# Retention followed by channel mix on one core: k transposed by head pairs, mu loaded as rows, block 0 split into parts, the last output tile by columns

## The chip, the cores and the metric

The kernel runs on one core of a Trainium2 chip. The core has a matrix engine (PE, with PEld for its weight loads), a vector engine (DVE), an activation engine (ACT), a general engine (POOL) and a queue engine (SP). Each engine takes its own instructions in program order and waits on semaphores for the others. Transfers between main memory and the on-chip memory are issued from SP, ACT or POOL; POOL's transfers here also convert float32 to float16. PE writes to PSUM, eight banks of 128 partitions by 2 KB, and DVE and ACT read them.

The metric is device time in microseconds (us) of one execution, as the median of several runs.

## What is computed

Two stages. The first is a retention recurrence over batch 4, 8 heads, 768 tokens, head size 64; the second is a channel mix with a shifted input, a squared relu and a sigmoid gate. The output is float32.

```python
# q, k, v: (4, 8, 768, 64)
gamma = 1.0 - 2.0 ** (-5.0 - np.arange(H))
for t in range(S):
    state = gamma[None, :, None, None] * state + np.einsum('bhd,bhe->bhde', k[:, :, t], v[:, :, t])
    y[:, :, t] = scale * np.einsum('bhd,bhde->bhe', q[:, :, t], state)
# x = y as (4, 768, 512); w_k: (512, 1024), w_v: (1024, 512), w_r: (512, 512)
x_prev = np.concatenate([np.zeros((B, 1, D)), x[:, :-1, :]], axis=1)
xk = mu_k * x + (1.0 - mu_k) * x_prev
xr = mu_r * x + (1.0 - mu_r) * x_prev
k = np.maximum(xk @ w_k, 0.0)
v = k * k @ w_v
r = 1.0 / (1.0 + np.exp(-(xr @ w_r)))
return r * v
```

## The kernel before

The 3072 tokens are cut into 12 blocks of 256 (three to a batch). Each block is two chunks u = 0, 1 of 128 tokens. A chunk's tokens lie two to a partition (index i), so that 64 partitions hold one chunk and 128 the block. The recurrence is done by chunks: inside a chunk by masked scores, between chunks by a decayed state.

Every step is a short function, called by a code in one long hand-over table, the string `ORDER` (lines 16 to 63). A word such as `X.0.0.1.2` is a code and its arguments; the digits behind `@` are the PSUM banks that the step uses. The table sets the order on every engine; what waits for what is put in as semaphores from the data. The first argument is the block n in all of them:

- `lk`, `lq`, `lv` (lines 169 to 179) load k, q and v. Loads of q and v go out on POOL, those of k on SP or, with a 2 behind the block, on POOL. `wk`, `wr`, `wv` load the weights on POOL, in halves for wk and wv; `mu` (393) loads the two mixing vectors on ACT, one value to a partition and column.
- `gy` (404) builds a decay table on DVE by a copy and seven doublings. `ks` (181) scales k into float16 by 128x1024 elements, on DVE (0) or POOL (1).
- `T` (195) transposes on PE by 64x64 pieces, 32 for q (0) and 32 for k (1), into two shared banks; `E` (207) copies the result out on ACT.
- `S` (222) makes the scores for i = 0, 1; `M` (234) masks them on DVE, 128x1024 each. `C` (244) makes each chunk's state product, `U` (262) adds it to the state on DVE, `G` (272) decays it on POOL. `I` (278) applies the state to q, `Y` (290) adds the masked scores times v, `D` (310) scales the result into xT on DVE.
- `dx` (318) takes the difference to the token before, on DVE or POOL. `X.n.w.j0.j1` (325) forms xk (w = 0) and xr (w = 1) on DVE, one 128x256 instruction for each j of 4.
- `K` (334) multiplies xk with w_k: four groups g of two, 8 matmuls of 256 columns each. `Q` (344) takes relu and square on ACT. `R` (351) makes the gate product by 128 tokens, 4 matmuls of 512; `s` (358) its sigmoid on ACT. `V` (363) multiplies with w_v by halves, 4 matmuls of 512 columns. `O` (370) joins gate and value on DVE, 128x512, and `st` (376) stores 256 KB from SP.
- `z` (397) are matmuls of zeros, whose results nothing reads.

Products of the same block are accumulated in PSUM, and rings of 2 to 6 buffers hold the tiles between the steps. All steps of block n+1's retention stand among the channel mix of block n.

## Time and profile before

| | us |
|---|---|
| median of 3 runs | 170.39 |
| lowest and highest of them | 169.95, 171.98 |
| profiled execution | 169.35 |
| its span, first to last instruction | 167.3 |

The profile shows one execution. A line of its timeline has the start and length in us, the engine, the source line, the operation with what it writes and reads, and in brackets how long the engine had stood idle and what ended that. Instructions of one kind that follow each other are merged, with their count; the length then runs from the first start to the last end. Ends of matmuls are modelled, so the distance between two starts tells more than a length. The chain of waits is followed back from the last instruction; "issue" in it is time in which an engine waited for nothing that the profile shows. In a table of windows, an engine's entry is its busy time in that stretch, with the number of instructions behind it, and PEclk is the granted share of PE's clock.

### The profile page before, as it was taken

What the parts mean: (1) busy time and instruction counts of PE and PEld (TensorE: products, weight loads), DVE (VectorE), ACT (ScalarE), POOL (GpSimd) and SP (SyncE); (2) the same over time, 40 slices, a digit from 0 to 9 for tenths busy, and PEclk for the clock granted to TensorE, in tenths of its full rate; (3) what the DMA queues carried; (4) which work ended last, traced back from release to release, by engine and by line L of the source; (5) the groups of instructions that cost most, each with busy time, mean ns of one, the idle gap of its engine ahead of it and who ended that gap; (6) DMA issues with size and microseconds to landing.
All of it is one profiled execution on the core that took longest, in us unless ns stands there. A gap on an engine that the chain in (4) does not pass through costs nothing.

```text
span 167.3 us, 6065 instructions
## 1 busy us (share of the span) xinstructions
PE 152.2 (91%) x2717; PEld 96.2 (57%) x2717; DVE 120.3 (72%) x194; ACT 93.5 (56%) x146; POOL 78.2 (47%) x75
## 2 busy tenths in 40 slices
PE   7884799989498969999999999999999999999990
PEld 2344446647365826756747756676566767566640
DVE  2676999696586999877877967977678699670311
ACT  3133009918145826776658738937657649286660
POOL 7984369395956952926809609114024140400000
PEclk9999579999789999999999999999999999999999
DMA  4999999999999991796569271630030030101303
GB/s 129 244 198 195 255 195 215 244 235 277 239 211 237 291 212 45 222 113 149 59 63 175 28 117 67 67 125 4 0 127 8 4 129 0 58 24 48 125 0 125
DMA packets 39529, 22.01 MB, mean 132 GB/s; under 512 B 26832, under 2 KB 35664, under 8 KB 39504
## 3 DMA queue, kind: packets, MB, share of 16 engines
q0 software_dynamic: 28464, 12.06, 53.2%
q1 hardware_dynamic: 9696, 9.44, 18.0%
q10 hardware_dynamic: 1344, 0.13, 1.2%
q8 instruction: 21, 0.34, 0.9%
q14 instruction: 4, 0.03, 0.0%
HBM read 24.25 MB, written 6.29 MB: 182 GB/s over the span
## 4 chain that ended last, share of the span: by engine, by line
PE 75%; DVE 9%; issue 5%; DMA 4%; ACT 2%; POOL 2%; DVEq 0%; POOLq 0%
PE ps L339 23%; PE ps L365 20%; PE ps L353 13%; DVE xr L329 5%; PE ps L228 4%; DMA k<-in_k_dram 4%; PE ps L298 4%; PE ps L202 4%; DVE a L236 3%; PE ps L399 2%; PE ps L255 2%; PE ps L285 2%; ACT k L349 1%; ACT kr L346 1%; DVE os L371 1%
## 5 line engine op out<-in xcount | busy, mean ns | idle before, releaser
L339 PE MATMUL ps<-xk,wk 128*128 128x256 f16 x384 | 47.8, 276 | 0.0
L365 PE MATMUL ps<-wv,k 128*128 128x512 f16 x192 | 44.6, 382 | 0.2 <-ACT k L349 0.2
L346 ACT ACTIVATE kr<-ps 128x512 f32<-128x512 f32 x48 | 28.4, 592 | 28.9 <-PE ps L339 28.9
L339 PEld LDWEIGHTS <-wk 128*128 128x128 f16 x384 | 37.0, 99 | 9.4 <-issue 0.2
L236 DVE TENSOR_TENSOR a<-ps,c_sb 128x1024 f16<-128x1024 f32 x24 | 28.5, 1219 | 10.5 <-PE ps L228 9.8
L349 ACT ACTIVATE k<-kr 128x512 f16<-128x512 f32 x48 | 30.3, 631 | 1.5
L365 PEld LDWEIGHTS <-k 128*128 128x128 f16 x192 | 18.6, 99 | 20.7 <-ACT k L349 2.1
L371 DVE SCALAR_TENSOR_TENSOR os<-ps,rs 128x512 f32<-128x512 f32 x24 | 16.4, 688 | 19.1 <-PE ps L365 8.0
L273 POOL TENSOR_TENSOR tg<-t,csm_sb 128x256 f16<-128x256 f32 x16 | 10.1, 629 | 37.0 <-DVE t L270 31.7
L353 PE MATMUL ps<-wr,xr 128*128 128x512 f16 x96 | 24.6, 380 | 1.9 <-DVE xr L329 1.4
L329 DVE SCALAR_TENSOR_TENSOR xr<-dx,mur,xT 128x256 f16<-128x256 f32 x48 | 25.3, 584 | 0.0
L320 POOL TENSOR_TENSOR dx<-xT 128x1024 f32<-128x1024 f32 x10 | 18.9, 1891 | 10.1 <-DVE xT L312 10.1
L359 ACT ACTIVATE rs<-ps 128x512 f32<-128x512 f32 x24 | 14.2, 590 | 16.8 <-PE ps L353 16.8
L329 DVE SCALAR_TENSOR_TENSOR xk<-dx,muk,xT 128x256 f16<-128x256 f32 x48 | 22.7, 533 | 1.1 <-POOL dx L320 1.0
L211 ACT COPY qT<-ps 128x1024 f16<-128x1024 f16 x12 | 12.1, 1010 | 19.1 <-PE ps L202 19.0
L183 POOL TENSOR_TENSOR ks<-k,csm_sb 128x1024 f16<-128x1024 f32 x10 | 19.3, 1927 | 0.9 <-POOL tg L273 0.8
L312 DVE TENSOR_TENSOR xT<-ps,gy_sb 128x1024 f32<-128x1024 f32 x12 | 14.7, 1223 | 3.4 <-PE ps L298 2.5
L170 POOL DMA_DIRECT2D q<-in_q_dram x12 | 10.9, 912 | 11.9 <-PE ps L202 9.9
L353 PEld LDWEIGHTS <-xr 128*128 128x128 f16 x96 | 8.6, 97 | 9.7 <-DVE xr L329 1.9
L228 PE MATMUL ps<-qT,kT 64*64 64x128 f16 x384 | 11.7, 227 | 2.6 <-issue 2.4
L170 POOL DMA_DIRECT2D v<-in_v_dram x12 | 11.0, 917 | 3.9 <-DMA wr<-in_moe_w_r_dram 2.1
L228 PEld LDWEIGHTS <-kT 64*64 64x64 f16 x384 | 8.2, 108 | 7.7 <-issue 4.5
(32 smaller groups left out, 119.2 us busy)
## 6 DMA issues: line engine op xcount, KB each, us to landing
out_dram<-os SPq DMA_DIRECT2D x24, 256.0 KB, 3.1
k<-in_k_dram SPq DMA_DIRECT2D x6, 512.0 KB, 4.7
q<-in_q_dram POOLq DMA_DIRECT2D x12, 256.0 KB, 8.6
v<-in_v_dram POOLq DMA_DIRECT2D x12, 256.0 KB, 6.8
k<-in_k_dram POOLq DMA_DIRECT2D x6, 512.0 KB, 13.8
wk<-in_moe_w_k_dram POOLq DMA_DIRECT2D x2, 512.0 KB, 10.6
wv<-in_moe_w_v_dram POOLq DMA_DIRECT2D x2, 512.0 KB, 17.1
wr<-in_moe_w_r_dram POOLq DMA_DIRECT2D x1, 512.0 KB, 13.7
```

Source lines behind the costliest of these rows:

```text
L170: eng.dma_start(out=d(n)[:, 2 * j0 : 2 * j1], in_=rows(x, n)[:, 2 * j0 : 2 * j1])
L183: (nc.vector, nc.gpsimd)[e].tensor_tensor(out=KS(n)[:, h0:h1].rearrange("p h (i d) -> p (h i) d", i=2), in0=K32(n)[:, h0:h1].rearrange("p ...
L228: nc.tensor.matmul(pa[u * D : u * D + D, hp, j, :], lhsT=KT(n)[r, u, j, i, :], rhs=QT(n)[r, u, j, :], start=(j == 0), stop=(j == NJ - 1), ...
L236: nc.vector.tensor_tensor(out=t[:, i], in0=pairs(banks("S", n, i)), in1=causal[:, i, None, None, :].to_broadcast([P, 2, NJ, C]), op=ALU.mult,)
L320: (nc.vector, nc.gpsimd)[e].tensor_tensor(out=DX(n)[:, j0:j1], in0=x[:, j0:j1, c : c + TM], in1=x[:, j0:j1, c - 1 : c + TM - 1], op=ALU.su ...
L329: nc.vector.scalar_tensor_tensor(out=XM[w](n)[:, j], in0=DX(n)[:, j], scalar=mu[:, j : j + 1], in1=x[:, j, c - 1 : c + TM - 1], op0=ALU.mu ...
L339: nc.tensor.matmul(pz[:, i, :], lhsT=wk16[:, co, fo * P : fo * P + P], rhs=XM[0](n)[:, co, :], start=(i == 0 and co == 0), stop=(co == NCO ...
L346: nc.scalar.activation(out=kr, in_=banks("K", n, g).rearrange("p (i t) -> p i t", i=2), func=AF.Relu)
L349: nc.scalar.activation(out=K2(n)[:, 2 * g : 2 * g + 2], in_=kr, func=AF.Square)
L353: nc.tensor.matmul(banks("R", n, tb), lhsT=XM[1](n)[:, co, tb * P : tb * P + P], rhs=wr16[:, co, :], start=(co == 0), stop=(co == NCO - 1),)
L365: nc.tensor.matmul(banks("V", n, tb, 0), lhsT=K2(n)[:, fo, tb * P : tb * P + P], rhs=wv16[:, fo, :], start=(fo == 0), stop=(fo == NFO - 1),)
L371: nc.vector.scalar_tensor_tensor(out=OS(2 * n + tb), in0=banks("V", n, tb, 0), scalar=1.0 / (KSC * KSC), in1=RS(2 * n + tb), op0=ALU.mult, ...
```

## The change

Five things are changed, and the table `ORDER` is written anew for all twelve blocks (its first words are shown in the diff).

1. *k by head pairs.* The scaled k lies as (i, head, d) and not as (head, i, d). One transpose takes a pair of heads, 128 tokens' partitions by 128 columns, so that a block's k takes 8 transposes of 128x128 and not 32 of 64x64. It lands in a bank of its own and is copied by its own step. q is still transposed by 64x64 (`Tq`), into two banks.
2. *mu from rows.* The two vectors are loaded as 4 rows of 128 each, transposed on PE (`mt`) and copied by ACT (`me`). They go out on ACT ahead of the first copies.
3. *Block 0 up to the scores by halves of heads.* Its k is loaded, scaled, transposed, copied, scored and masked in two halves (`.0.2` and `.2.4`).
4. *Block 0 from y to the key products by chunks.* `Du`, `du`, `Xu`, `Ku` and `Qu` do a chunk of 128 tokens each. A `Ku` is 16 matmuls of 128 columns.
5. *The last tile by columns.* The values, the result and the store of the last 128 tokens go by two halves of 256 columns, the stores from SP and ACT.

All loads of k behind block 0's go out on POOL. wk's first half is issued right behind v of block 0, and wk, wr and wv stand ahead of block 2's loads. The scaling of block 2's k is moved from POOL to DVE. There are 38 matmuls of zeros and not 29.

```diff
-lk.0 lq.0 lv.0 gy lk.1.2 lq.1 lv.1 wk.0 ks.0.0 wk.1 z.13@0 T.0.0@01 wr T.0.1 lk.2.2 E.0.0 C.0@23
...
+lk.0.0.0.2 lk.0.0.2.4 lq.0 mu lv.0 gy wk.0 lk.1.2 ks.0.0.0.2 z.7@0 mt@0 lq.1 me ks.0.0.2.4
+T.0.1.0.2@1 lv.1 E.0.1.0.2 T.0.1.2.4@0 E.0.1.2.4 wk.1 z.2@2 Tq.0@23 wr E.0.0 wv.0 z.4@4
...
-    gk_np = gam[None, :, None] ** (C - 1 - tok[:, None, :])
+    gk_np = gam[None, None, :] ** (C - 1 - tok[:, :, None])
...
-    KS = ring("ks_", 3, [H, 2 * D], F16)
-    QT = ring("qT_", 3, [2, NJ, C], F16)
-    KT = ring("kT_", 3, [2, NJ, 2, D], F16)
+    KS = ring("ks_", 3, [2, H, D], F16)
+    QT = ring("qT_", 3, [NJ, 2, C], F16)
+    KT = ring("kT_", 3, [NJ, 2, C], F16)
...
-            out=KS(n)[:, h0:h1].rearrange("p h (i d) -> p (h i) d", i=2),
-            in0=K32(n)[:, h0:h1].rearrange("p h (i d) -> p (h i) d", i=2),
-            in1=gk[:, 2 * h0 : 2 * h1, None].to_broadcast([P, 2 * (h1 - h0), D]),
+            out=KS(n)[:, :, h0:h1],
+            in0=K32(n)[:, h0:h1].rearrange("p h (i d) -> p i h d", i=2),
+            in1=gks[:, :, h0:h1, None].to_broadcast([P, 2, h1 - h0, D]),
...
     def trans(n, a, j0=0, j1=NJ):
-        pt, src = turned(n), (Q16, KS)[a](n)
+        pt = turned(n, a, j0).rearrange("p (j i t) -> p j i t", j=NJ, i=2)
         for j in range(j0, j1):
+            for i in range(2):
+                if a:
+                    nc.tensor.transpose(
+                        pt[:, j, i], KS(n)[:, i, 2 * j : 2 * j + 2].rearrange("p h d -> p (h d)"),
+                        ident,
+                    )
...
-    def scores(n, i):
-        pa = pairs(banks("S", n, i))
-        for j in range(NJ):
+    def scores(n, i, j0=0, j1=NJ):
+        pa = pairs(banks("S", n, i, j0))
+        for j in range(j0, j1):
...
+    def yout_u(n, u):
+        x, c = col(n)
+        nc.vector.tensor_tensor(
+            out=x[:, :, c + u * C : c + u * C + C], in0=pairs(banks("I", n))[:, u], in1=gy,
+            op=ALU.mult,
+        )
...
+    def mixed_in(n, w, j0, j1, t0, t1):
         x, c = col(n)
-        mu = (muk, mur)[w]
         for j in range(j0, j1):
             nc.vector.scalar_tensor_tensor(
-                out=XM[w](n)[:, j], in0=DX(n)[:, j], scalar=mu[:, j : j + 1],
-                in1=x[:, j, c - 1 : c + TM - 1], op0=ALU.mult, op1=ALU.add,
-            )
+                out=XM[w](n)[:, j, t0:t1], in0=DX(n)[:, j, t0:t1],
+                scalar=mu[:, w * NCO + j : w * NCO + j + 1],
+                in1=x[:, j, c - 1 + t0 : c - 1 + t1], op0=ALU.mult, op1=ALU.add,
+            )
...
+    def keys_u(n, g, u):
+        pz = banks("Ku", n, g, u).rearrange("p (i t) -> p i t", i=4)
+        for i in range(4):
+            fo = 4 * g + i
+            for co in range(NCO):
+                nc.tensor.matmul(
+                    pz[:, i, :], lhsT=wk16[:, co, fo * P : fo * P + P],
+                    rhs=XM[0](n)[:, co, u * C : u * C + C],
+                    start=(i == 0 and co == 0), stop=(co == NCO - 1), skip_group_check=True,
+                )
...
+    def values_c(n, tb, c):
+        x = slice(c * dm // 2, (c + 1) * dm // 2)
+        for fo in range(NFO):
+            nc.tensor.matmul(
+                banks("Vc", n, tb, c)[:, x], lhsT=K2(n)[:, fo, tb * P : tb * P + P],
+                rhs=wv16[:, fo, x], start=(fo == 0), stop=(fo == NFO - 1), skip_group_check=True,
+            )
...
+    def store_c(n, tb, c, e):
+        x = slice(c * dm // 2, (c + 1) * dm // 2)
+        b, t0 = n // NB, n % NB * TM + tb * P
+        (nc.sync, nc.scalar)[e].dma_start(out=out[b, t0 : t0 + P, x], in_=OS(2 * n + tb)[:, x])
...
     def load_mu():
-        nc.scalar.dma_start(out=muk, in_=moe_mu_k.rearrange("(co ci) -> ci co", ci=P))
-        nc.scalar.dma_start(out=mur, in_=moe_mu_r.rearrange("(co ci) -> ci co", ci=P))
+        for w, x in enumerate((moe_mu_k, moe_mu_r)):
+            nc.scalar.dma_start(
+                out=mu8[w * NCO : (w + 1) * NCO], in_=x.rearrange("(co ci) -> co ci", ci=P)
+            )
+
+    def trans_mu():
+        nc.tensor.transpose(banks("mt")[:, 0 : 2 * NCO], mu8[0 : 2 * NCO], ident8)
+
+    def copy_mu():
+        nc.scalar.copy(out=mu, in_=banks("mt")[:, 0 : 2 * NCO])
```

What the new table makes of the order is shown at two places. The first is DVE at the start of the program, from the first scaling of k (ks) to xk and xr of block 0; a is the masked scores, tg and t the state, xT the scaled result, dx the difference. The numbers behind a name are buffers. Before:

```order
L183 TENSOR_TENSOR ks_74<-k_0_70,csm_sb 128x1024
L266 TENSOR_TENSOR tg_91<-ps,csm_sb 128x256
L270 TENSOR_TENSOR t_1_87<-ps,tg_91 128x256
L183 TENSOR_TENSOR ks_75<-k_1_71,csm_sb 128x1024
L236 TENSOR_TENSOR a_0_83<-ps,c_sb 128x1024 x2
L270 TENSOR_TENSOR t_2_88<-ps,tg_92 128x256
L312 TENSOR_TENSOR xT_128<-ps,gy_sb 128x2x4x128
L236 TENSOR_TENSOR a_1_84<-ps,c_sb 128x1024 x2
L320 TENSOR_TENSOR dx_96<-xT_128 128x1024
L329 SCALAR_TENSOR_TENSOR xk_98<-dx_96,muk,xT_128 128x256 x4
L329 SCALAR_TENSOR_TENSOR xr_101<-dx_96,mur,xT_128 128x256 x4
```

And DVE at the same place now, up to the last xk of block 0's first chunk:

```order
L189 TENSOR_TENSOR ks_74<-k_0_70,csm_sb 128x2x256 x2
L253 TENSOR_TENSOR a_0_83<-ps,c_sb 128x2x256 x2
L283 TENSOR_TENSOR tg_91<-ps,csm_sb 128x256
L287 TENSOR_TENSOR t_1_87<-ps,tg_91 128x256
L253 TENSOR_TENSOR a_0_83<-ps,c_sb 128x2x256 x2
L189 TENSOR_TENSOR ks_75<-k_1_71,csm_sb 128x1024
L337 TENSOR_TENSOR xT_128<-ps,gy_sb 128x4x128
L344 TENSOR_TENSOR dx_96<-xT_128 128x4x128
L358 SCALAR_TENSOR_TENSOR xr_101<-dx_96,mu,xT_128 128x128 x4
L358 SCALAR_TENSOR_TENSOR xk_98<-dx_96,mu,xT_128 128x128 x3
L253 TENSOR_TENSOR a_1_84<-ps,c_sb 128x1024
L358 SCALAR_TENSOR_TENSOR xk_98<-dx_96,mu,xT_128 128x128
```

Block 0's masks now stand ahead of block 1's scaled k, xr stands ahead of xk, and one of block 1's two masks stands ahead of the last xk of the first chunk; the other has moved behind all of the second chunk.

The second place is POOL's queue of loads at the start, where k, q, v carry the buffer and wk, wr, wv are the weights. Before:

```order
L170 DMA q_0_62<-in_q_dram 128x8x128
L170 DMA v_0_66<-in_v_dram 128x8x128
L170 DMA k_1_71<-in_k_dram 128x8x128
L170 DMA q_1_63<-in_q_dram 128x8x128
L170 DMA v_1_67<-in_v_dram 128x8x128
L415 DMA wk_125<-in_moe_w_k_dram 128x4x512 x2
L418 DMA wr_127<-in_moe_w_r_dram 128x4x512
L170 DMA k_2_72<-in_k_dram 128x8x128
```

And POOL at the same place now:

```order
L176 DMA q_0_62<-in_q_dram 128x8x128
L176 DMA v_0_66<-in_v_dram 128x8x128
L499 DMA wk_125<-in_moe_w_k_dram 128x4x512
L176 DMA k_1_71<-in_k_dram 128x8x128
L176 DMA q_1_63<-in_q_dram 128x8x128
L176 DMA v_1_67<-in_v_dram 128x8x128
L499 DMA wk_125<-in_moe_w_k_dram 128x4x512
L502 DMA wr_127<-in_moe_w_r_dram 128x4x512
L506 DMA wv_126<-in_moe_w_v_dram 128x4x512
L506 DMA wv_126<-in_moe_w_v_dram 128x4x512
L176 DMA k_2_72<-in_k_dram 128x8x128
```

One half of wk has moved ahead of block 1's loads, and both halves of wv ahead of block 2's k.

More of the change, by code (lines that the diff above doesn't have):

```diff
@@ L135 @@
     c16 = const.tile([P, 3 * P], F16, name="c16_sb")
-    csm = const.tile([P, 2 * H + (2 + LOG) * NJ], F32, name="csm_sb")
+    csm = const.tile([P, 2 * H + (2 + LOG) * NJ + 2 * NCO], F32, name="csm_sb")
     gy = const.tile([P, NJ, C], F32, name="gy_sb")
     zero = const.tile([P, 512], F16, name="zero")
-    muk = const.tile([P, NCO], F32, name="muk")
-    mur = const.tile([P, NCO], F32, name="mur")
+    mu8 = const.tile([P, P], F32, name="mu8")
+    mu = const.tile([P, 2 * NCO], F32, name="mu")
     wk16 = const.tile([P, NCO, dff], F16, name="wk16")
@@ L334, in keys, with squared_u @@
+    def squared_u(n, g, u):
+        kr = KR(next(relus)).rearrange("p a (b t) -> p (a b) t", t=C)
+        nc.scalar.activation(
+            out=kr, in_=banks("Ku", n, g, u).rearrange("p (i t) -> p i t", i=4), func=AF.Relu
+        )
+        nc.scalar.activation(
+            out=K2(n)[:, 4 * g : 4 * g + 4, u * C : u * C + C], in_=kr, func=AF.Square
+        )
     def keys(n, g):
@@ L436 @@
         if at:
-            key = {"T": args[:1], "I": args[:1]}.get(code, args)
-            BANK[(code,) + key] = [int(x) for x in at]
+            key = args
+            if code in ("T", "Tq"):
+                code_key, key = "T", (args[0], args[1] if code == "T" else 0, (args[2:] + (0,))[0])
+            else:
+                code_key = code
+                key = {"I": args[:1], "S": args[:2] + (args[2:] + (0,))[:1]}.get(code, args)
+            BANK[(code_key,) + key] = [int(x) for x in at]
         CODES[code](*args)
```

188 lines of the change are left out of this document (107 added, 81 removed).

## The prediction

> **What bounds the kernel now.** I read the page's busy times and slices first, then a table of windows, then the chain of waits in order of time, and last the timelines of DVE and POOL in the first 65 us. The page's line of busy times, its slices of PE and of PE's clock:
>
> ```profile
> PE 152.2 (91%) x2717; PEld 96.2 (57%) x2717; DVE 120.3 (72%) x194; ACT 93.5 (56%) x146; POOL 78.2 (47%) x75
> ...
> PE   7884799989498969999999999999999999999990
> ...
> PEclk9999579999789999999999999999999999999999
> ```
>
> The windows (us from the start; busy time by engine; clock; DMA share; GB/s):
>
> ```profile
> 42.00:46.00 4.00, 1.86 (x17) 1.32 (x17) 2.24 (x3) 0.55 (x1) 4.00 (x5) 0.72 1.32 233
> ...
> 56.00:62.80 6.80, 5.42 (x35) 3.09 (x33) 6.80 (x9) 3.46 (x6) 4.79 (x4) 1.00 1.35 256
> ...
> 80.00:100.00 20.00, 19.84 (x381) 13.03 (x377) 15.61 (x28) 12.20 (x20) 9.64 (x9) 1.00 0.63 89
> 100.00:120.00 20.00, 20.00 (x365) 13.36 (x353) 16.22 (x27) 15.20 (x24) 7.71 (x6) 1.00 0.25 55
> ```
>
> The chain of waits (start, length, what; the longest pieces up to 63 us, three from the steady part, and the last):
>
> ```profile
> 21.16 3.10 PE ps L399 x9
> 24.27 1.75 PE ps L339 x16
> ...
> 41.92 2.22 issue
> ...
> 44.67 1.82 PE ps L339 x8
> 46.49 2.12 PE ps L365 x8
> ...
> 50.72 0.44 issue
> ...
> 53.49 0.87 PE ps L339 x8
> ...
> 57.19 4.68 DVE xr L329 x4
> ...
> 62.73 1.90 PE ps L353 x8
> ...
> 76.22 0.58 PE ps L202 x64
> ...
> 81.41 2.62 PE ps L339 x24
> 84.03 3.45 PE ps L365 x16
> ...
> 163.30 0.69 DVE os L371
> ```
>
> From 63 us on PE is the bound: 19.84 and 20.00 of 20 us busy. Only what changes PE's own work counts there. Ahead of that, two stretches are not PE's. Up to 24.27 it does some retention and fills with zeros (nine from 21.16), since DVE has not made xk. Between 36 and 63 it pauses: 2.22 us at 41.92 on "issue", then the clock falls (0.72 in the window from 42), so that 8 key matmuls take 1.82 where they take 0.87 at 53.49, and 8 value matmuls 2.12 where half of the 16 at 84.03 take 1.73; 0.44 at 50.72; and 6.80 - 5.42 = 1.38 before 62.73, where the gate waits for xr. These are 2.22 + 0.95 + 0.39 + 0.44 + 1.38 = 5.4 us.
>
> **The start.** DVE's timeline before, with POOL's load issues left out:
>
> ```profile
> 4.11 1.85 DVE L408 TENSOR_TENSOR gy_sb<-gy_sb,csm_sb 128x4 f32<-128x4 f32 x7
> 5.88 1.22 DVE L183 TENSOR_TENSOR ks<-k,csm_sb 128x1024 f16<-128x1024 f32 x1
> 8.73 0.42 DVE L266 TENSOR_TENSOR tg<-ps,csm_sb 128x256 f16<-128x256 f32 x1 [1.63 <-PE ps L255]
> ...
> 10.06 1.59 DVE L183 TENSOR_TENSOR ks<-k,csm_sb 128x1024 f16<-128x1024 f32 x1 [0.38 <-DMA k<-in_k_dram]
> 11.57 2.35 DVE L236 TENSOR_TENSOR a<-ps,c_sb 128x1024 f16<-128x1024 f32 x2
> ...
> 19.61 1.22 DVE L320 TENSOR_TENSOR dx<-xT 128x1024 f32<-128x1024 f32 x1
> 20.87 1.67 DVE L329 SCALAR_TENSOR_TENSOR xk<-dx,muk,xT 128x256 f16<-128x256 f32 x4
> 22.45 1.67 DVE L329 SCALAR_TENSOR_TENSOR xr<-dx,mur,xT 128x256 f16<-128x256 f32 x4
> ```
>
> 1024 columns take 1.22 and 256 take 0.42, so 512 take 0.69 on the line between. Four xk take 1.58 from start to start, 0.395 each; for 128 columns the bounds are 0.20 (half) and 0.395 (no saving); the line for 512 has a fixed share of 0.15, so I take 0.26. The decay table ends at 5.96 as before and gates the scaling; halves bring the first k at 6.65 and not 7.10. But PE now also waits for mu's load, which stands ahead of k's transposes; and q's transposes and its copy, which had come first, come last. The first masks start between 10.4 (a half of the scores that before began at 10.08) and 11.6 (mu 1 us late); I take 10.9, against 11.57. Then DVE, in the new order: four half masks 2.76, two state steps 0.84, block 1's scaling 1.26, half result 0.69, half difference 0.70, eight of 128 columns 2.1, one mask 1.23: 9.6 us; 0.4 for POOL's work beside it (block 1's scaling took 1.59 and not 1.22). The first key product starts at 20.9, not at 24.3.
>
> This gain does not stay whole. DVE still has the second chunk (state 0.42, result 0.69, difference 0.70, eight 2.1, with 0.4 for POOL), the other mask of block 1, a state step, block 1's result and difference (1.23 + 0.42 + 1.23 + 1.26), its xr 1.6, block 2's scaling 1.26 that was POOL's, xk 1.6 and a state step 0.42. With 0.9 for POOL and 0.4 for PE's turn that is 14.6 us: block 1's xk is whole at about 35.5, and PE, by its order, ends the second key group of block 1 at 38.2. Until then PE has from 20.9: 64 key matmuls of 128 columns 3.5, four gates 3.45, block 0's values 3.45, two key groups 1.75, retention of blocks 1 and 2 3.0; 15.2 of 17.3 us. At 36.3 the kernel before had done the same but for block 1's two gates (1.73) and one key group (0.87), and it paused 0.5 there: it is at this point at 36.8 + 2.6 = 39.4. So the start is worth 1.2 us (39.4 - 38.2), with 3.4 at most (the first key product's lead) and -1.0 if the masks start at 11.6 and small instructions cost more.
>
> **Loads.** POOL's rows in the kernel before, where it waits for a landing, and two scalings with DVE's rows beside them:
>
> ```profile
> 23.16 0.89 POOL L170 DMA_DIRECT2D k<-in_k_dram  x1 [0.99 <-DMA k<-in_k_dram]
> ...
> 30.87 0.89 POOL L170 DMA_DIRECT2D k<-in_k_dram  x1 [1.62 <-DMA wv<-in_moe_w_v_dram]
> ...
> 33.78 2.07 POOL L183 TENSOR_TENSOR ks<-k,csm_sb 128x1024 f16<-128x1024 f32 x1
> ...
> 58.87 1.92 POOL L183 TENSOR_TENSOR ks<-k,csm_sb 128x1024 f16<-128x1024 f32 x1
> ```
> ```profile
> 32.86 3.27 DVE L329 SCALAR_TENSOR_TENSOR xr<-dx,mur,xT 128x256 f16<-128x256 f32 x3
> ...
> 57.11 4.77 DVE L329 SCALAR_TENSOR_TENSOR xr<-dx,mur,xT 128x256 f16<-128x256 f32 x4
> ```
>
> Block 2's k had landed by 23.2 and the last half of wv by 30.9. Put behind wv (as the order has it), block 2's k lands about two wv halves later, at 28 to 29; its scaling comes at about 32. The same bytes pass by 31, so nothing behind is later. I cost it at nothing; if it slips past 32, DVE and all of block 1's xk wait for it. Five more loads of k are issued on POOL at 0.89 each; POOL is 47% busy.
>
> **The middle.** Of the 5.4 us I expect 1.5 to remain: by the new order PE waits about 0.4 for block 2's xr, 0.7 for block 3's xk, 0.4 for copies. The "issue" pauses are PE running out of instructions. The page's queue of instructions:
>
> ```profile
> q8 instruction: 21, 0.34, 0.9%
> ```
>
> 0.34 MB in 21 packets for PE's 2 x 2717 instructions is some 256 in each. Counted in PE's order, the pauses at 41.92 and 50.72 stand at instructions 1472 and 1728, 256 apart. Ahead of 1472, 256 instructions ran within 4 us. Now PE has 4959 and not 5436, and the stretches of 256 in the middle (to the masked products of block 2, the state of block 4, the scores of block 4) each hold 6 to 7 us of PE's work. Without the pause the clock does not fall either. 5.4 - 1.5 = 3.9 gained; bounds 0.5 (the pauses return elsewhere) and 5.4.
>
> **PE's own work.** The 64 small transposes of a block take 0.58 (at 76.22), so k's 32 take 0.29. No transpose of 128x128 was run before. The nearest row is the key matmul of 256 columns: 2.62 / 24 = 0.109 each; half is 0.055, the whole is the upper bound. The weight load must keep up:
>
> ```profile
> L339 PEld LDWEIGHTS <-wk 128*128 128x128 f16 x384 | 37.0, 99 | 9.4 <-issue 0.2
> ...
> L202 PEld LDWEIGHTS <-ks 64*64 64x64 f16 x384 | 4.2, 106 | 0.7 <-issue 0.4 <-DVE ks L183 0.2
> ```
>
> A full load takes no longer (99 ns) than a 64x64 one (106 ns) of which 32 pass in 0.29 us, so I take 0.057: 8 make 0.455, 0.165 more for each block. For blocks 3 to 11 that is 9 x 0.165 = 1.5 us lost (1.4 to 5.2). The Trainium skill (TensorE: Matmul & The Clock Gate, section Back-to-back issue gap) speaks against the change: it gives about 81 ns a matmul for a stream of weight loads and matmuls of 128 columns. By it the loss would be 9 x (0.65 - 0.29) = 3.2 us and the sum 1.7 us higher, an estimate; no run here shows such a stream yet.
>
> **The end.** The last result on DVE takes 0.69 for 512 columns; on 256 it takes 0.42 by the row at 8.73, and its store is half as large: 0.4 gained (0.2 to 0.7). 16 value matmuls of 256 columns at 0.109 make 1.75 against 1.73 for 8 of 512. Nothing else there.
>
> **The sum.** -1.2 (start) - 3.9 (middle) + 1.5 (transposes) - 0.4 (end) = -4.0 us. The profiled execution took 169.35 with a span of 167.3; it becomes 165.35 with 163.3. The median of the runs, 170.39, lies 1.04 above the profiled execution; the same distance gives 166.4, 2.3% below the median before. A measurement of this kernel tells about 2%, 3.4 us, from no change.
>
> **Rivals.**
> 1. Small matmuls keep a floor. If a pair of weight load and matmul of 128 columns takes some 80 ns (between the bounds 55 and 109), block 0's 64 key matmuls cost 1.6 more, half of it beside DVE's work, and the transposes 1.7 to 1.9 more: +2.6, 169.0, within 2%. For it: no such row exists, and weight loads are 57% busy. Against: loads of 64x64 pass at 9 ns each. The rule of the Trainium skill above is of this kind. Chance 0.20.
> 2. The pauses come back at other places. One pause of 2.22 with the fall of the clock (1.34) costs 3.6: 170.0, within 2%. For it: the fetch boundary is every 256 instructions whatever the order, and loads run to 60 us as before. Against: fewer instructions, and retention spread thinner. Chance 0.15.
> 3. Slower: DVE starves PE in the first 65 us because POOL holds it up. At 32.86 three xr took 3.27 where three take 1.2, while POOL scaled k; at 57.11 four took 4.77, not 1.6. Such a collision costs 2.1 to 3.2 us. All loads of k now pass POOL, so its scalings stand at other times. To be slower by 2% (173.8) it takes 7.4 more than my sum, three collisions more than I count, all on the path. 0.11, with 174.5.
> 4. More gain: no pause remains (-1.5) and the start keeps 2.2: 163.9, faster. Chance 0.12.
>
> **How the numbers follow.** My forecast, 166.4, has 0.42, all of it on the faster side of 167.0. With rival 4 faster has 0.54; rivals 1 and 2 give 0.35 for within 2%; slower 0.11. The range has to leave out two in ten: the slower rival and the better part of rival 4 with the bounds of the start: 162.5 to 171.5. It holds rivals 1 and 2 and one collision.
>
> **What would show it.** In the profile after: the first key product (128x128 of xk) at 20.9, within 1; block 1's last xk at 35.5; no "issue" above 1 us between 36 and 63 and a full clock there; 8 transposes of k at 57 ns from start to start; 128x128 scaled-tensor instructions at 0.26; PE solid from 65 on, and its last matmul at 159.6. It is wrong if the first key product starts past 23, if the transposes take 80 ns, or if PE waits over 3 us on DVE between 30 and 65.

## The result, and the profile after

| | before | after |
|---|---|---|
| median us (4 runs each) | 170.51 | 164.1 |
| lowest and highest | 169.95, 171.98 | 163.25, 164.16 |
| ratio of the medians, 95% interval | | 0.9626, 0.9585 to 0.9666 |
| profiled execution | 169.35 | 164.16 |
| its span | 167.3 | 162.4 |

The change makes the kernel 3.7% faster. The forecast was 166.4 us, between 162.5 and 171.5, faster with a chance of 0.54. Some executions, most of them of the kernel before, run in a slower state of the chip: here and below the ratios compare the fast ones only, the medians count all, and the profile of b_pair below is of one counted as slow (169.15 us).

The page after: busy times, slices of PE and of PE's clock. The share of PE rose from 91% to 95%, and the clock is full in every slice.

```profile
PE 153.6 (95%) x2479; PEld 99.4 (61%) x2479; DVE 116.5 (72%) x209; ACT 94.3 (58%) x148; POOL 80.5 (50%) x79
...
PE   7499999999999999999969999999999999999992
...
PEclk9999999999999999999999999999999999999999
```

The windows that the prediction showed, and one more, in the same columns:

```profile
36.00:42.00 6.00, 5.84 (x178) 4.76 (x177) 4.95 (x7) 4.85 (x8) 6.00 (x6) 1.00 1.52 263
42.00:46.00 4.00, 4.00 (x61) 2.39 (x58) 2.44 (x3) 2.73 (x4) 4.00 (x5) 1.00 1.46 237
...
56.00:62.80 6.80, 6.80 (x125) 4.58 (x124) 6.04 (x13) 3.55 (x6) 5.42 (x6) 1.00 1.11 213
...
80.00:100.00 20.00, 18.38 (x312) 11.75 (x307) 16.24 (x24) 10.58 (x18) 9.23 (x9) 1.00 0.68 106
100.00:120.00 20.00, 20.00 (x326) 12.73 (x316) 15.46 (x27) 13.35 (x21) 5.27 (x4) 1.00 0.21 42
```

From 42 to 46 the clock was 0.72 and is 1.00; from 56 to 62.8 PE is busy throughout, where it had waited 1.38. But from 80 to 100 PE now stands still for 1.6 us. PE's timeline after has that wait, and the head and the tail of the program:

```profile
6.46 0.24 PE L476 MATMUL ps<-csm_sb,mu 8*128 8x8 f32 x1 [2.10 <-DMA mu<-in_moe_mu_r_dram]
6.63 1.03 PE L204 MATMUL ps<-c_sb,ks 128*128 128x128 f16 x8
...
21.36 1.14 PE L375 MATMUL ps<-xk,wk 128*128 128x128 f16 x16
...
84.41 1.80 PE L395 MATMUL ps<-xk,wk 128*128 128x256 f16 x15 [1.62 <-DVE xk L358]
...
157.26 1.91 PE L439 MATMUL ps<-wv,k 128*128 128x256 f16 x16
```

DVE's timeline after: one 128x128 step of xr takes 1.06 / 4 = 0.265 (from 17.83 to 18.89), block 1's xk is whole at 35.64, and the xk that PE waits for at 84 takes 4.33 where four take 1.58 from start to start (78.45 to 80.03, for xr).

```profile
17.83 1.14 DVE L358 SCALAR_TENSOR_TENSOR xr<-dx,mu,xT 128x128 f16<-128x128 f32 x4
18.89 0.87 DVE L358 SCALAR_TENSOR_TENSOR xk<-dx,mu,xT 128x128 f16<-128x128 f32 x3
...
35.16 0.48 DVE L358 SCALAR_TENSOR_TENSOR xk<-dx,mu,xT 128x256 f16<-128x256 f32 x1
...
78.45 1.66 DVE L358 SCALAR_TENSOR_TENSOR xr<-dx,mu,xT 128x256 f16<-128x256 f32 x4
80.03 4.33 DVE L358 SCALAR_TENSOR_TENSOR xk<-dx,mu,xT 128x256 f16<-128x256 f32 x4
...
85.75 0.67 DVE L427 SCALAR_TENSOR_TENSOR os<-ps,rs 128x512 f32<-128x512 f32 x1
```

Beside it, POOL's timeline after: two load issues, and the scaling of block 10's k within the 4.33 us.

```profile
80.38 0.88 POOL L176 DMA_DIRECT2D v<-in_v_dram  x1 [1.18 <-PE ps L271]
81.24 0.89 POOL L176 DMA_DIRECT2D q<-in_q_dram  x1
82.13 1.93 POOL L189 TENSOR_TENSOR ks<-k,csm_sb 128x1024 f16<-128x1024 f32 x1
...
85.97 1.89 POOL L344 TENSOR_TENSOR dx<-xT 128x1024 f32<-128x1024 f32 x1 [0.58 <-DVE xT L329]
```

The chain of waits after: the longest "issue" between 36 and 63 us, a key group of block 0 and k's eight transposes of a later block:

```profile
25.96 0.89 PE ps L375 x16
...
51.68 0.51 issue
...
107.48 0.45 PE ps L204 x8
```

To see where the time went, I give each kind of matmul one weight in both kernels (the time between two starts; k's 8 transposes together the weight of the 32 of before; zeros none) and ask when the same sum of work has been started. The differences are the lead of the new kernel:

| reached before at | after at | lead |
|---|---|---|
| 38.7 | 37.4 | 1.4 |
| 62.7 | 57.3 | 5.5 |
| 79.0 | 73.7 | 5.3 |
| 91.9 | 88.1 | 3.8 |
| 159.6 | 155.5 | 4.1 |
| 167.3 (end of the span) | 162.4 | 4.9 |

The end of the span is the row of the page itself. So 1.4 us come from the start and 4.1 from the middle; 1.6 are given back at 82 us; the rest of the steady part gives nothing back, and the end brings 0.8. The value at the start is that of one execution: by the profile of a_same, the same kernel once more (below), the lead at the first row is 2.3, and from there to the second 4.2.

### The profile page after: what moved, and what is told of

It reads as the page before. It is cut to its first block, busy times and chain, and to the rows that moved or that the text cites. A ratio compares the mean times of both kernels' runs of the same rounds, so it can differ in the third digit from the quotient of the medians.

```text
span 162.4 us, 5592 instructions
## 1 busy us (share of the span) xinstructions
PE 153.6 (95%) x2479; PEld 99.4 (61%) x2479; DVE 116.5 (72%) x209; ACT 94.3 (58%) x148; POOL 80.5 (50%) x79
## 4 chain that ended last, share of the span: by engine, by line
PE 81%; DVE 7%; ACT 5%; DMA 2%; issue 1%; ACTq 1%; POOL 0%; DVEq 0%
PE ps L395 23%; PE ps L421 22%; PE ps L409 12%; PE ps L246 5%; PE ps L483 4%; PE ps L315 3%; PE ps L204 3%; PE ps L302 3%; DMA mu<-in_moe_mu_r_dram 2%; DVE xk L358 2%; PE ps L222 2%; ACT qT L238 2%; PE ps L271 2%; ACT kr L402 1%; PE ps L375 1%
## 5 line engine op out<-in xcount | busy, mean ns | idle before, releaser
L395 PE MATMUL ps<-xk,wk 128*128 128x256 f16 x352 | 44.1, 273 | 1.7 <-DVE xk L358 1.6
L395 PEld LDWEIGHTS <-wk 128*128 128x128 f16 x352 | 33.4, 98 | 10.2 <-issue 2.1
L253 DVE TENSOR_TENSOR a<-ps,c_sb 128x1024 f16<-128x1024 f32 (+1 forms) x26 | 28.8, 1138 | 13.3 <-PE ps L246 6.5
L402 ACT ACTIVATE kr<-ps 128x512 f32<-128x512 f32 x44 | 26.1, 593 | 18.0 <-PE ps L395 18.0
L344 POOL TENSOR_TENSOR dx<-xT 128x1024 f32<-128x1024 f32 x10 | 18.9, 1892 | 20.3 <-DVE xT L329 20.3
L405 ACT ACTIVATE k<-kr 128x512 f16<-128x512 f32 x44 | 27.7, 630 | 1.4
L358 DVE SCALAR_TENSOR_TENSOR xr<-dx,mu,xT 128x256 f16<-128x256 f32 (+1 forms) x52 | 21.0, 465 | 4.0 <-POOL dx L344 3.9
L358 DVE SCALAR_TENSOR_TENSOR xk<-dx,mu,xT 128x256 f16<-128x256 f32 (+1 forms) x52 | 23.4, 510 | 0.0
L189 POOL TENSOR_TENSOR ks<-k,csm_sb 128x1024 f16<-128x1024 f32 x9 | 17.1, 1905 | 5.1 <-PE ps L271 5.1
L238 ACT COPY kT<-ps 128x1024 f16<-128x1024 f16 (+1 forms) x13 | 12.1, 940 | 8.7 <-PE ps L204 8.7
L483 PE MATMUL ps<-zero 128*128 128x512 f16 x38 | 13.0, 480 | 1.2 <-DVE xT L467 1.2
```

What stands on the lines that cost most here:

```text
L189: (nc.vector, nc.gpsimd)[e].tensor_tensor(out=KS(n)[:, :, h0:h1], in0=K32(n)[:, h0:h1].rearrange("p h (i d) -> p i h d", i=2), in1=gks[:, ...
L238: nc.scalar.copy(out=out, in_=pt)
L253: nc.vector.tensor_tensor(out=A2(n)[:, i, :, j0:j1], in0=pairs(banks("S", n, i, j0))[:, :, j0:j1], in1=causal[:, i, None, None, :].to_broa ...
L344: (nc.vector, nc.gpsimd)[e].tensor_tensor(out=DX(n)[:, j0:j1, t0:t1], in0=x[:, j0:j1, c + t0 : c + t1], in1=x[:, j0:j1, c - 1 + t0 : c - 1 ...
L358: nc.vector.scalar_tensor_tensor(out=XM[w](n)[:, j, t0:t1], in0=DX(n)[:, j, t0:t1], scalar=mu[:, w * NCO + j : w * NCO + j + 1], in1=x[:, ...
L395: nc.tensor.matmul(pz[:, i, :], lhsT=wk16[:, co, fo * P : fo * P + P], rhs=XM[0](n)[:, co, :], start=(i == 0 and co == 0), stop=(co == NCO ...
```

## The experiments

Twelve kernels were run, four at a time beside the kernel before: the first four rows on one chip, the next four on a second and the last four on a third. Times are medians in us; the ratio is to the kernel before on the same chip, with its 95% interval. Between rows of different chips the ratios are the ones to compare.

| run | what it is | us | before | ratio |
|---|---|---|---|---|
| b_grid | before, PE's instructions shifted by 224 | 172.99 | 170.21 | 1.014 (1.004 to 1.024) |
| a_grid | after, shifted by 144 | 163.35 | 170.21 | 0.965 (0.959 to 0.971) |
| a_mt | after, mu's transpose later | 160.72 | 170.21 | 0.951 (0.945 to 0.958) |
| a_tail | after, last tile whole | 162.28 | 170.21 | 0.959 (0.954 to 0.964) |
| a_same | after itself | 163.27 | 170.85 | 0.961 (0.956 to 0.967) |
| a_chunk | after, part 4 undone | 166.18 | 170.85 | 0.977 (0.971 to 0.983) |
| a_half | after, part 3 undone | 162.78 | 170.85 | 0.958 (0.953 to 0.963) |
| a_pad | after, 24 small products a block put back | 169.51 | 170.85 | 0.994 (0.989 to 0.998) |
| b_pair | before with part 1 alone | 169.03 | 170.81 | 0.989 (0.984 to 0.994) |
| a_ks | after, one scaling moved | 161.38 | 170.81 | 0.953 (0.945 to 0.960) |
| a_mtks | both | 160.98 | 170.81 | 0.948 (0.943 to 0.953) |
| a_best | both, and xk ahead of xr at the start | 161.16 | 170.81 | 0.949 (0.944 to 0.954) |

a_same itself began earlier than the profiled execution of the result: its first key product starts at 20.49, not 21.36, though mu's load ended PE's wait only 0.14 us earlier. So profiles of one kernel can differ by 0.9 us at the start, and single profiles decide nothing smaller there.

### The pause in the middle: is it PE's supply of instructions?

The first two runs keep all the work and change only the count of PE's instructions, by more and narrower products of zeros.

```diff
-    def zeros(count):
+    def zeros(count, n=512):
...
+                banks("z", *((count, n) if n != 512 else (count,)))[:, 0:n], lhsT=zero[:, 0:P],
+                rhs=zero[:, 0:n], start=True, stop=True, skip_group_check=True,
...
-z.13@0
+z.101.64@0
...
-z.9@2
+z.33.128@2
```

> The kernel before, with more but narrower matmuls of zeros ahead of the first key product: 101 of 64 columns for 13 of 512, and 33 of 128 columns for 9 of 512. It adds 112 matmuls with their weight loads, 224 instructions on PE, and about the same PE time. Theory 'supply' (PE pauses where 256 of its instructions are used up faster than the next 256 are fetched): the boundaries move by 224 instructions to places where about 5 us lie between them; no pause above 1 us is left between 36 and 56 us, the clock stays full in 42 to 48, and the time falls by 2.5 to 4 us against the kernel before (166.5 to 168). Rival 'wait' (the pause at 41.9 us is a wait for data or a bank that the profile does not show): the pause stays in the second scores of block 3, and the time stays within 1 us of the kernel before.

The kernel became 1.4% slower, where a gain had been expected, and the pauses moved. The chain of waits of b_grid:

```profile
14.86 0.33 PE ps L298 x9
15.19 2.36 issue
...
43.91 0.76 PE ps L339 x6
44.67 2.42 issue
```

The pause that had stood ahead of block 3's scores (L228) at 41.92 stands in a group of key products (L339) at 44.67, and a second one has come into block 0's masked products (L298). Counted in PE's order (a matmul and its weight load are two) both stand where an instruction 192 + 256 m begins (704 and 1728), as the pauses before did (448, 1472, 1728). So the place follows the count; it is no wait for data. That the pause would go, or shrink, was not borne out: it was only moved.

The same shift in the changed kernel, whose first seven zeros became 79 of 64 columns (`z.7@0` to `z.79.64@0`):

> The changed kernel, with the first 7 matmuls of zeros of 512 columns replaced by 79 of 64 columns, which adds 144 instructions on PE while it waits for mu anyway. Theory 'supply': one boundary falls into block 2's and 3's retention where only 4.2 us lie between two boundaries, and a fetch with its lag took 4.9 us there: a pause of 0.5 to 0.9 us near 41 us, the clock stays full, and the time grows by 0.3 to 1.0 us (164.5 to 165.2). Rival 'wait': no pause there, time unchanged within 0.3 us.

The time shows nothing, 0.965 against 0.961 for the changed kernel, but the trace does. PE's timeline of a_grid:

```profile
40.55 0.45 PE L221 MATMUL ps<-c_sb,q 64*64 64x64 f16 x32 [0.16 <-ACT kr L401]
42.45 1.05 PE L394 MATMUL ps<-xk,wk 128*128 128x256 f16 x8 [1.45 <-DVE xT L328]
```

DVE's timeline of a_grid, with the xT that is named there:

```profile
40.52 1.23 DVE L328 TENSOR_TENSOR xT<-ps,gy_sb 128x1024 f32<-128x1024 f32 x1 [0.69 <-ACT kr L401]
```

xT was done at 41.75, 0.7 us before PE went on, so it is not what ended the wait; and in a_same the same key group starts at 40.54, while that xT runs from 40.14 to 41.36, so it does not need it at all. PE stops at instruction 1472, 192 + 5 x 256, and the piece with it was fetched from 40.04 to 41.05. The shift has brought a pause of 1.45 us into the changed kernel. The time hides it, since a loss at another place fell away in this run (PE is busy throughout from 80 to 100 us; more below). So the changed kernel owes its quiet middle to its count too.

`z.24.64` ahead of k's transposes in blocks 1 to 6 brings PE's count there back to that of before, by products of zeros of 64x64:

```diff
+            for c in range(count):
+                r = slice(c % 2 * D, c % 2 * D + D)
+                nc.tensor.matmul(
+                    banks("z", count, n)[r, 0:n], lhsT=zero[0:D, 0:D], rhs=zero[0:D, 0:n],
+                    start=True, stop=True, skip_group_check=True,
+                )
...
-T.3.1@7
+z.24.64@7 T.3.1@7
```

> The changed kernel with 24 products of zeros of 64x64 ahead of k's transposes in blocks 1 to 6, so that PE has as many instructions a block there as before (8 + 24 = 32), at about 0.01 to 0.03 us each. Nothing reads them. Theory A (the pause of 2.2 us in the middle came because PE had eaten 256 instructions faster than the next 256 were brought, and it went because k's transposes are 24 fewer a block): a pause of 1 us or more on issue stands again between 30 and 65 us, with the clock below full behind it, and the time rises by 1.5 to 4 us over the changed kernel's. Rival B (the pause went because the loads or the waits around it were moved by the new order, not by the count): no such pause, and the time rises by no more than the products' own 24 x 6 x 0.01 to 0.03 = 1.4 to 4 us in all where PE is the bound, of which blocks 1 to 3 lie beside DVE's work: under 1.5 us. The chain of waits tells the two apart, not the time alone.

169.51 us: 6.2 above the changed kernel by the medians and 5.6 by the ratios (0.994 against 0.961), and most of the gain is gone. PE's timeline of a_pad has the pause:

```profile
41.69 0.45 PE L221 MATMUL ps<-c_sb,q 64*64 64x64 f16 x32
44.99 1.05 PE L394 MATMUL ps<-xk,wk 128*128 128x256 f16 x8 [2.85 <-issue]
```

Its windows show PE busy for 1.15 of 4 us there, and its DMA queues from 41.9 to 43.6 show one packet of instructions in just that time:

```profile
42.00:46.00 4.00, 1.15 (x28) 0.92 (x13) 1.15 (x1) 1.21 (x2) 3.10 (x4) 1.00 1.58 246
```
```profile
q8 instruction: 1, 0.02, 3.4%
```

The pause stands at instruction 1472 again, 192 + 5 x 256. PE had passed the boundary before at 38.22 and needed the next piece at 41.94; it was fetched from 42.59 to 43.53. In a_same the same boundaries are passed at 39.40 and 46.32, and the piece has been there since 43.58. The zeros' own cost is six times 0.38 = 2.3 us; against a_same the lead falls by 0.6 up to 38.7 us and by 4.5 more up to 62.7. This is the theory of the supply, and the rival (the new order alone) falls. The time missed the upper end of 4 us, since I had not added the zeros' own time to the pause; without the 2.3 about 3.3 are left, which is what the supply is worth here.

### Part 1 alone

b_pair has the order, loads and zeros of before, and only k's layout, with its eight transposes put into the upper halves of the two banks that q's use.

```diff
-T.0.0@01 wr T.0.1 lk.2.2 E.0.0
+Tq.0@01 wr Th.0 lk.2.2 E.0.0
...
+    def trans_k(n):
+        for j in range(NJ):
+            for i in range(2):
+                nc.tensor.transpose(
+                    upper(n)[:, j // 2, j % 2, i],
+                    KS(n)[:, i, 2 * j : 2 * j + 2].rearrange("p h d -> p (h d)"), ident,
+                )
```

> The kernel before with part 1 alone: k's transposes by head pairs (8 and not 32 a block), in the order, with the loads, banks and zeros of before. Theory A (the pause in the middle came from PE's instructions running out; fewer of them remove it): no pause on issue of 1 us or more between 36 and 63 us and a full clock there; the start as before (first key product at 24.3, within 0.4), no change after 63 us but 0.2 us more a block, 1.8 in all; the time 2.2 + 1.3 us of pause and slow clock and 0.4 less, 1.8 more: some 168.5 us, ratio 0.98 to 1.0, against 0.961 for all five parts. Rival B (the pause follows the loads or a wait, not the count): a pause of 1.5 us or more stays, and the time is 170.5 us or more.

169.03 us, as the theory had it (168.5, ratio 0.98 to 1.0). The windows of b_pair:

```profile
42.00:46.00 4.00, 4.00 (x59) 2.80 (x52) 2.99 (x4) 2.41 (x4) 4.00 (x4) 1.00 1.34 242
46.00:50.00 4.00, 3.46 (x118) 2.33 (x116) 4.00 (x5) 2.33 (x4) 3.07 (x3) 1.00 1.47 209
...
56.00:62.80 6.80, 5.17 (x28) 2.02 (x29) 6.80 (x11) 2.25 (x4) 2.98 (x3) 1.00 1.33 255
```

The long pause is gone and the clock is full; 0.54 us remain near 47. But 1.63 are lost between 56 and 62.8, where the gate waits for xr as before. Measured as above, b_pair leads by 3.2 us when the kernel before is at 48.6, by 2.05 at 58.2, and by 0.19 at 159.6: the larger transposes take 1.9 back over some nine blocks, 0.2 a block at most, as some 0.25 of it is b_pair's longer wait for xr (1.63 against 1.38). Part 1 alone is worth 1.1%, the five together 3.7 to 3.9%.

### Block 0: chunks and halves

a_chunk replaces `Du`, `du`, `Xu`, `Ku`, `Qu` by the whole steps:

```diff
-Du.0.0
+D.0
...
-du.0.0.0
+dx.0.0
...
-Xu.0.1.0.0.1
+X.0.1.0.1
...
-Ku.0.0.0@4 Du.0.1
+K.0.0@4
...
-Ku.0.1.0@0 Xu.0.1.1.0.1 Xu.0.1.1.2.3
+K.0.1@0
...
-Ku.0.1.1@5
+K.0.2@5
...
-Ku.0.0.1@1
+K.0.3@1
```

> Part 4 undone: block 0 goes from y to the key products whole again (one result and one difference of 1024 columns, xr and xk of 256 columns, key groups of 256 columns), all else as in the changed kernel. Theory A (DVE sets the start, and block 1's xk is the point where PE and DVE meet, whatever block 0 does in between): DVE's fixed shares are saved, about 2 x (0.15 + 0.12) + 8 x 0.125 = 1.5 us of DVE's work, so block 1's xk is whole about 1 us earlier although block 0's first key product starts about 2 to 3 us later (near 24); PE's products of block 0 that had stood in that gap move behind, and the time is within 1 us of the changed kernel's, 163.3 to 165.1. Rival B (the early first key product is what the change earns at the start): 2 us or more are lost, 166 us and up.

My theory missed: 166.18 us, 2.9 above the changed kernel. The first key product does not start near 24 but at 20.03; its group then waits 1.26 for xk. PE's timeline of a_chunk:

```profile
21.95 0.81 PE L392 MATMUL ps<-xk,wk 128*128 128x256 f16 x6 [1.26 <-DVE xk L355]
...
40.98 0.26 PE L219 MATMUL ps<-c_sb,q 64*64 64x64 f16 x8 [0.16 <-ACT kr L399]
42.38 0.38 PE L219 MATMUL ps<-c_sb,q 64*64 64x64 f16 x24 [1.14 <-issue]
```

And DVE's, where it now waits for PE's masked products of block 1:

```profile
28.04 1.22 DVE L326 TENSOR_TENSOR xT<-ps,gy_sb 128x1024 f32<-128x1024 f32 x1 [2.81 <-PE ps L312]
...
35.11 0.48 DVE L355 SCALAR_TENSOR_TENSOR xk<-dx,mu,xT 128x256 f16<-128x256 f32 x1
```

DVE did have less work, but it stood idle for 2.81 us, because PE reaches block 1's masked products only behind block 0's first three key groups. Block 1's xk is whole at 35.59, and at 34.78 in a_same. PE's order and DVE's row bind each other there; DVE does not set the start alone. By the lead, 0.8 of the 2.9 are lost by 38.7 us. The other 2.0 are lost from there to 62.7, where the pauses on issue (1.14 at 42.38, 0.6 more near 55) stand at instructions 1216 and 1728: with 32 products fewer the boundaries fall on faster stretches. So the rival's 2 us came, for the larger part by another way than the rival's.

a_half replaces the halves of heads by whole steps (`lk.0`, `ks.0.0`, `T.0.1@1`, `S.0.0@23`, `M.0.0` and so on):

> Part 3 undone: block 0 is loaded, scaled, transposed, copied, scored and masked whole again, all else as in the changed kernel. Theory A: the first masks start 0.3 to 0.6 us later and DVE saves four fixed shares of 0.12 to 0.15, so the first key product is 0 to 0.3 us later and the time 0 to 0.3 us longer than the changed kernel's. Rival B (the halves carry the start, as the first copy and mask run beside the second half's load): 1 us or more is lost, and the first key product starts past 22.3.

162.78 us against 163.27, and the first key product at 20.54 against 20.49. Part 3 is worth nothing that can be measured here; the theory holds.

### mu's place, and the last tile

a_mt moves mu's transpose and copy behind those of q:

```diff
-z.7@0 mt@0 lq.1 me ks.0.0.2.4
+z.7@0 lq.1 ks.0.0.2.4
...
-wr E.0.0
+wr E.0.0 mt@7 me
```

> The changed kernel with mu's transposition and copy moved behind q's transposes of block 0 on PE and behind its copy on ACT. Theory 'gate' (at the start PE waits for mu's load, 2.1 us up to 6.46, while the scaled k is there at 5.8): the transposes of k start near 5.8, the first key product near 20.4 and not at 21.4, and the time falls by 0.5 to 1.0 us (163.1 to 163.6). Rival 'q' (the start is set by q's landing at 7.5 and by the zeros behind it): the first key product moves by less than 0.4 us and the time by less than 0.3.

160.72 us, the lowest median of all. k's first transposes start at 5.89, when the first half of k is scaled, and no longer behind mu's load (2.10 us of idle PE in the rows above); the first key product starts at 20.02. The wait of 1.6 us for xk was gone too, which none of this had foreseen and which is the larger part of the gain: by the lead over a_same 0.9 us stand at 38.7 and 2.7 behind that wait.

a_tail has the last tile whole (`V.11.1.0@1 ... O.11.1 st.11.1` in place of `Vc`, `Oc`, `sc`):

> The changed kernel with the last 128 tokens' values, result and store whole, as before. Theory 'tail' (the split by columns is worth what the last result and the store get shorter): from PE's last matmul to the end of the span 4.0 and not 3.2 us, time 0.5 to 0.9 us longer (164.6 to 165.0). Rival: what is won behind PE is lost by the 16 smaller value matmuls, or the store's fixed time hides it: within 0.3 us.

162.28 us, no difference in time from the changed kernel. By the rows the columns earn 0.5: from the first of the last tile's matmuls to the end of the span 5.1 us pass in the changed kernel (157.26 to 162.4) and 5.7 in a_tail. The runs cannot show so little, above all as the profiled execution of a_tail (164.3 us, with the wait for xk in it) is 2 us above its own median.

### The wait at 82 us

a_ks takes block 10's scaling of k from POOL, where the rows above show it beside DVE's xk, to DVE behind block 6's first result.

```diff
-X.5.0.3.4 U.7.0 ks.10.1 D.6
+X.5.0.3.4 U.7.0 D.6
...
-s.7.0 O.6.0 K.7.1@1
+s.7.0 O.6.0 ks.10.0 K.7.1@1
```

> The changed kernel with one step moved: block 10's scaling of k goes from POOL (where it ran beside DVE's xk at 79 to 83 us) to DVE, behind the first result of block 6. Theory A (DVE's xk was held while POOL computed, and PE waited 1.6 us for it): the wait of 1.6 us for xk is gone, the four xk take 1.6 us and not 4.3, DVE's 1.2 us are covered by its idle time, and the time is 1.4 to 1.7 us below the changed kernel's, 161.7 us or 0.951. Rival B (DVE was held by the two load issues, or PE would have waited for the next thing): the wait stays or comes again within 20 us, and the time is within 0.5 us of the changed kernel's.

161.38 us, 1.9 below a_same's median, and 1.4 by the ratios (0.953 against 0.961). The four xk take their normal time, and PE is busy throughout from 80 to 100 us. DVE's timeline and a window of a_ks:

```profile
78.90 1.67 DVE L357 SCALAR_TENSOR_TENSOR xk<-dx,mu,xT 128x256 f16<-128x256 f32 x4
```
```profile
80.00:100.00 20.00, 20.00 (x279) 13.10 (x277) 14.86 (x24) 12.06 (x21) 9.39 (x9) 1.00 0.72 109
```

Up to 62.7 us its lead over a_same is 0.3, behind the wait 2.0. The rival falls: nothing took the wait's place.

a_mtks has both edits, a_best also xk ahead of xr in block 0's first chunk, with fewer zeros ahead of the first key product (`z.7@4` to `z.1@4`).

> The changed kernel with mu's transpose and copy behind q's (as in the earlier run of that edit, whose wait for xk in the middle was also gone) and with block 10's scaling on DVE as in the run before this one. Theory A (the two edits earn at separate places: some 1.0 us at the start, 1.6 at 81 us, which the earlier edit had escaped only by where its start put it): 160.5 us, 0.944 to 0.95, the same as that edit alone. Rival B (they add): 159.2 us or less.

> As the run before it, and xk of block 0's first chunk stands ahead of xr on DVE (as in the kernel before), with three groups of zeros cut to fit: 1 and not 7 ahead of the first key product, 3 and not 4 ahead of the first scores. Theory A (PE takes up the first two key products 1 us earlier, and the gates still wait for xr at the old time): the first key product at 18.8 us and not 20.0, and 0.5 to 1 us of it kept, since block 1's masked products, for which DVE waited 0.8 us, come earlier: 159.5 to 160 us. Rival B (DVE's row of work sets block 1's xk whatever PE does in between): within 0.3 us of the run before.

160.98 and 161.16 us: neither differs from a_mt. The first was as expected; the second was not, its 0.5 to 1 us did not come. a_mt had escaped the collision (its four xk take 1.58 us from start to start beside the same load issues), so the edits do not add. In a_best the first key product starts at 19.16, and PE then waits; its timeline:

```profile
19.16 1.06 PE L374 MATMUL ps<-xk,wk 128*128 128x128 f16 x16
21.68 0.30 PE L301 MATMUL ps<-qT,tg 64*64 64x128 f16 x4 [1.47 <-POOL tg L289]
```

Block 1's xk is whole at 34.3 in both (33.81 and 33.85, and 0.48 long). So these versions beat both kernels, by 5% against before; the intervals of a_mtks (0.943 to 0.953) and a_best (0.944 to 0.954) do not overlap that of the changed kernel, 0.956 to 0.967. What the edit of a_mt alone is worth at the start is not settled: by the lead at 38.7 it is 0.9 us against a_same, but 0.2 for a_mtks against a_ks, and 0.4 by the medians of these two.

## Why the prediction was right

It was right in its sign, and its sum was near: a span of 162.4 for 163.3. Two terms that were wrong by about 1.5 us each cancelled, one put too high (the transposes) and one left out (the wait at 82 us): that part is luck.

- *Start, -1.2: measured -1.4.* The first key product came at 21.36 (20.9), block 1's xk at 35.64 (35.5), the small scaled-tensor steps at 0.265 (0.26). That most of the early lead of 2.9 us does not stay was right. What a_chunk added: DVE is not alone in setting that point. And one cause was overlooked: the kernel before pauses at its start too, at instruction 448, and DVE waits for the product behind that pause. The chain of waits and DVE's timeline before:

```profile
13.10 1.57 issue
```
```profile
15.14 0.42 DVE L270 TENSOR_TENSOR t<-ps,tg 128x256 f32<-128x256 f32 x1 [1.23 <-PE ps L255]
```

The prediction put that stretch down to DVE's work alone. The changed kernel has no pause there, so up to 1.2 us of the early lead can come from the supply of instructions; no run separates that from the new order of DVE and of the loads, neither of which was put back by itself.

- *Middle, -3.9: measured -4.1.* No issue over 0.51 us, full clock, no wait for xr. That 1.5 us of waits would remain was wrong: from 36 to 63 us PE stands still for 0.25 us in all, so some 5.1 of the 5.4 went, as in the first half of rival 4 (whose 163.9 us is nearer than my own sum). The 4.1 holds the larger transposes of blocks 3 to 5 as well (3 x 0.165 = 0.5), and 0.5 more that no run explains; the near hit of this term is in part luck. The reason given, PE out of instructions, is the one that a_pad and b_grid show, and rival 2 (the pauses come back) did not happen in this order; a_grid, a_chunk and a_pad show that it takes little to bring them back: 144 instructions more at the start, 64 fewer in block 0, or 48 more a block.
- *Transposes, +1.5: this term was mis-sized in the sum, though its price was right.* Eight take 0.45 us (56 ns each; I took 57), the 16 key products 0.89 (56 ns), and b_pair shows 0.2 lost a block. By the Trainium skill (TensorE: Matmul & The Clock Gate, section Back-to-back issue gap) a stream at 128 columns takes about 81 ns; the trace does not agree here, and rival 1 falls with it. But in the changed kernel the lead does not fall in the steady part (3.8 at 91.9 us, 4.1 at 159.6). Something that I had put at nothing, how the other matmuls stand in blocks 3 to 11, earns about as much as the transposes cost. From 100 to 140 us the masked products stand 17.1 ns apart on the mean (before 20.3), the gates 217 (223), the scores 21.3 (23.0) and the value products 223 (229, with one wait of 0.34 us for ACT in it): 0.3 us a block less. The state's products (12.9 for 9.9), q's transposes (9.9 for 8.5) and the key products (112.8 for 111.1) give 0.18 of that back; what is left is about the transposes' price. These means count the change to the next kind of matmul, so they depend on which kinds follow each other. b_pair, with the large transposes in the order of before, has the masked products at 20.7 and the gates at 223, so it is the new table and not k's layout that packs them closer. The scores stand at 19.9 there, so theirs is not the table's; before they hold a pause of 0.3 us at instruction 4544 (125.87 us). Which of the table's moves does it no run tells apart.
- *The wait at 82 us, not in the sum: +1.6.* Rival 3 had this mechanism, DVE held up by POOL's scaling, with a price of 2.1 to 3.2 us, but placed it in the first 65 us; there it did not occur. I had said PE would be solid from 65 on, and that is the step that failed. a_ks shows the cause and the price.
- *End, -0.4: measured -0.8* by the lead, of which a_tail gives 0.5 to the columns.

The miss in the median, 166.4 for 164.1, is 0.9 of span, 0.3 of time around the span (2.05 before, 1.76 after), and 1.1 because I added the 1.04 us by which the median before lay above the profiled execution, while the profiled execution after lies at its median. That offset was the worst-founded number of the sum: one execution's distance says nothing of another kernel's.

## What to carry to other kernels

Count an engine's instructions, not only its time: where loads fill the DMA queues, a stretch in which PE eats 256 instructions in less than some 6.5 us can stop it for 0.5 to 3 us, so fewer and larger instructions pay even where each one costs more. When an edit takes or adds instructions, look where the boundaries fall before a gain or a loss is put down to the edit itself. And after a new order is written, look in the steady part for POOL's steps beside steps of DVE that read the on-chip memory twice: moving one of them (a_ks) earned 1.4 to 1.9 us.

## What was not expected of the hardware

The fetch of PE's instructions is slow to start while loads run: 2.5 to 3.7 us after PE has passed the boundary before in a_same up to 60 us (39.40 to 42.65), 3.0 to 4.7 in a_pad and 3.3 to 7.2 before (these two with one exception each behind 57 us, 1.0 us and none); from 72 us on it often takes 0.5 to 1.1, and in a_same some fetches begin up to 1.3 us ahead of the boundary. The slow one there in a_same, 3.0 us (79.07 to 82.09), falls under two loads that move 0.5 MB. In nine of the profiles a fetch with no load or store moving in the microsecond ahead of it came at most 1.6 us late, and the later ones stood beside loads, though some beside loads came at once. The fetch then runs for about 1 us, and PE goes on 1.2 to 1.6 us after the piece has landed (a_pad: 43.53 and 44.99). So the pause follows from how fast PE eats a piece. Worked out from the traces, near 40 us:

| run | from boundary to boundary, us | pause at its end, us |
|---|---|---|
| before | 38.11 to 41.71, 3.6 | 2.2 |
| a_pad | 38.22 to 41.94, 3.7 | 2.9 |
| a_grid | 36.61 to 40.80, 4.2 | 1.5 |
| a_chunk | 36.65 to 41.04, 4.4 | 1.1 |
| b_pair | 40.99 to 47.00, 6.0 | 0.5 |
| a_same | 39.40 to 46.32, 6.9 | none |

So the lag goes with the loads, but no run tried loads that leave more room.

A step of DVE that reads two operands from the on-chip memory (SBUF) can stand still until a POOL step is over. Of the four xk at 80 us in the changed kernel three take 0.48 each, beside a load issue of POOL. The fourth begins at 81.22, just ahead of POOL's next load issue (81.24), and ends 0.3 us behind POOL's scaling (84.06); DVE's timeline in a narrow window:

```profile
81.22 3.15 DVE L358 SCALAR_TENSOR_TENSOR xk<-dx,mu,xT 128x256 f16<-128x256 f32 x1
```

A step with one operand from PSUM was not held: the result at 85.75 took 0.67 beside POOL's difference from 85.97. The Trainium skill (SBUF — State Buffer, section SBUF: two separate sides) says that such a DVE step and a POOL step that reads this memory lock each other out for a whole instruction: the one that starts first goes through and the other waits. The rows agree as to which steps are held, but not as to which of the two waits, since the step that was held began 0.9 us ahead of POOL's scaling. In seven profiles the fourth xk begins 0.03 us ahead of the same load issue: it was held in five (the changed kernel, a_same, a_half, a_tail and a_chunk) and not in two (a_mt and a_grid). So the place alone does not decide it, and what does no run shows.
